# Stores of gates and operands begun by GpSimd, and feed-forward quarters in alternating direction with four pieces kept

## The chip, the cores and the metric

The kernel runs on one core of a Trainium2 chip. The metric is device time in microseconds (us), and the time of a version is the median of its runs. One further execution was recorded by the hardware profiler, and all views below are of that one. The engines are PE (TensorE), DVE (VectorE), ACT (ScalarE), POOL (GpSimd) and SP (SyncE, which in the version before begins every data transfer). Each engine executes its own instructions strictly in order: an instruction that waits holds up all those behind it on the same engine.

## The reference, cut to what matters

```python
# q, k, v: (8, 8, 576, 64); 4608 tokens of 512 features after the heads are joined
scores = matmul(q_c, k_c.T) / sqrt(64)          # chunks of 64 tokens
attn = exp(scores - max); attn /= sum + 1e-9
x = matmul(attn, v_c)                            # -> (8, 576, 512)
xn = (x - mean) / sqrt(var + 1e-6) * g_ln
x2 = x + maximum(xn @ w_ch1, 0) @ w_ch2          # 512 -> 2048 -> 512
gate = sigmoid(causal_conv(x2, conv_w))          # 5 taps, each feature by itself
out = (gate * (x2 @ w_val)) @ w_out
```

## The kernel before, in words

The 4608 tokens are worked in nine blocks (`b` = 0 to 8) of 512, and attention in 36 units of 128 tokens. The feed-forward layer's 2048 inner features are four quarters (`g`) of 512. Blocks 0 and 1 go through it in the plain way. From block 2 on (`hidden`) a quarter's first layer is done in seven products (called "2", "1", "6", "5", "3", "7", "4") of sums of a quarter of the weights with sums of the activations, which takes the place of eight plain products. A product is twelve matmuls at L1255 (`twelve`). The seven accumulate in two PSUM banks: 1, 6, 7 and 4 in bank a, which the instruction lists name m1, and 2 in bank b, which is then opened anew for 5 and 3 (m2 and m5). Between certain products ACT copies a bank (L1347) or DVE adds one to a copy (L1354): product 6 waits for the copy after 1, product 3 for the one after 5, product 4 for DVE's sum after 7. The second layer's matmuls (L1412 to L1414, called y groups here, three matmuls of 512 columns each) are independent of these and fill the time in between, as do the attention units' bursts (L631) and transposes (L604).

The sums of the weights are made once, written to HBM (`a_dram[g, m]`, 512 KB each) and loaded again for each block (L1327): 7 blocks x 4 quarters x 7 pieces = 196 loads, into a ring of six rooms (`RING`). A load waits until the product six before it has read its room.

After a block's feed-forward layer, `conv` computes the gate's five taps for four groups of 128 features, on ACT (the first, L1638) and DVE (four, L1645), in two rooms u0 and u1 (`u_room`). Each result is stored to HBM (`gate_dram`, L1658) and its room is used again two groups later. `seven` splits the block's output into seven operands for the later gated projection, on ACT (L1472) and DVE (L1477), in three rooms (`SPLITS`), and stores each to `x7_dram` (L1482). These stores are begun by SP, the engine that begins the loads of pieces. `conv_again` and `seven_again` do the same for block 0 out of x2 stored earlier (L1600, L1525).

The order on every engine is set before the launch by a small planner (`Plan.run`): each operation has an engine, a duration and a priority (`pri`), is offered when its predecessors are done, and the engine takes the one with the lowest number. A successor is offered after the planner's `HOP` of the engine (3500 ns for SP, 200 for POOL) plus the operation's `more`, and, where the predecessor ran on SP, plus the successor's own `slack`. These figures decide the order alone; on the chip the instructions wait on semaphores. POOL before has little to do: an attention unit's 1/sqrt(variance) (`rstd`, L770), on which DVE's normalisation (L789) and then PE's transposes (L604) wait, and some copies (L826).

Of the kernel before, what the change touches and what calls it, by code (L numbers as in the profile page):

```python
# [31 lines left out]
class Plan:  # L32
# [23 lines left out]
    def run(self):  # L56
        for op in self.ops:
            op.left = len(op.deps)
            for d in op.deps:
                d.after.append(op)  # L60
        free = {e: 740.0 if e == "SP" else 0.0 for op in self.ops for e in op.eng}
        ready = {e: [] for e in free}
        events = []
        done = set()

        def offer(op):
            for e in op.eng:
                heapq.heappush(ready[e], (op.pri, op.seq, op))

        for op in self.ops:  # L70
            if not op.left:
                offer(op)
        t, n, moved, landed = 0.0, 0, 0.0, []
        while n < len(self.ops):
            for e in free:
                if free[e] > t:
                    continue
                q = ready[e]
                while q and q[0][2].seq in done:
                    heapq.heappop(q)  # L80
                if not q:
                    spent = self.idle(t) if self.idle and e == "PE" else None
                    if spent:
                        free[e] = t + spent
                        heapq.heappush(events, (free[e], -1, None))
                    continue
                op = heapq.heappop(q)[2]
                done.add(op.seq)
                dur = op.dur[op.eng.index(e)] if isinstance(op.dur, tuple) else op.dur
                end = t  # L90
                for x, parts in op.xfer or ():
                    flying = landed[-self.LANES :]
                    if len(flying) == self.LANES:
                        end = max(end, flying[0][0])
                    for l, _ in flying:
                        if sum(m for z, m in flying if z > end) + parts > self.RING:
                            end = max(end, l)
                    turn = self.TURN if parts == P and landed and landed[-1][1] != P else 0.0
                    end += dur
                    moved = max(end + self.LAG, moved + turn) + x  # L100
                    landed.append((moved, parts))
                if not op.xfer:
                    end = t + dur
                free[e] = end
                if len(op.eng) > 1:
                    op.fn(e)
                else:
                    op.fn()
                n += 1
                for a in op.after:  # L110
                    if op.xfer:
                        wait = moved - end
                    else:
                        wait = 0.0 if a.eng == (e,) else max(self.HOP[e], self.HOP["PE"] if "PE" in a.eng else 0.0) + op.more
                        if e == "SP":
                            wait += a.slack
                    a.ready = max(a.ready, end + wait)
                    a.left -= 1
                    if not a.left:
                        heapq.heappush(events, (a.ready, a.seq, a))  # L120
                heapq.heappush(events, (free[e], -1, None))
            if n == len(self.ops):
                break
            t = max(t, events[0][0])
            while events and events[0][0] <= t:
                op = heapq.heappop(events)[2]
                if op is not None:
                    offer(op)
# [3 lines left out]
def chunk_attention_ffn_gated_conv(  # L132
# [1176 lines left out]
        last = [s6, s5, split("7", q12, t3, t2), split("4", q21, t4), t1, t4]  # L1309
        hold("xs", *last)  # L1310

    def hidden(b, g):

        n = NG * (b - SB) + g
        pri = when[b, 4 * g] - 9000.0
        ta, tb = f"h{n % 2}", f"h{1 - n % 2}"
        opens, closes = g == 0, g == NG - 1
        st, w = {}, {}
        two_f = 2 * P

        def product(m, into, new, deps):
            rt = RING[ring_n[0] % len(RING)]
            ring_n[0] += 1

            def load():
                w[m] = slot(rt, [P, 2, 2, two_f], F32R, f"a{b}_{g}_{m}")
                nc.sync.dma_start(out=w[m].bitcast(F32), in_=a_dram[g, m].bitcast(F32))  # L1327

            def go():
                if new:  # L1330
                    st[into] = bank(tb if into == "b" else ta, f"m{m}_{b}_{g}").rearrange("p (f x) -> p f x", f=2)
                x = operand(m)
                twelve(st[into], lambda s, k: w[m][:, s, k], lambda s, k: x[:, s, k], new)

            at = pri + 1400.0 * MS.index(m)
            ld = add("SP", 1300, load, [a_store[g, m]] + take(rt), at - 16000.0)
            ld.more = 1500.0
            o = add("PE", 1410, go, [ld, B_op[b, m]] + deps, at)
            hold(rt, o)
            if g == NG - 1:  # L1340
                hold(f"o{m}", o)
            return o

# [11 lines left out]

            return add("DVE", 700, go, deps, pri - 1e7)

        m2 = product("2", "b", True, take(tb))
        m1 = product("1", "a", True, take(ta))
        s1 = shot("a", "hh0", m1)  # L1360
        c11 = join("hh0", "b", ALU.add, s1, m2)
        m6 = product("6", "a", False, [m1, s1])
# [69 lines left out]
    def seven(b, quad, reads, pri):  # L1432

        st, last = {}, {}
        HB = NB // 2

        def mix(to, x, y, *deps):


            def side(q):
                return [(0, HB, st["t"][:, :, :HB])] if q is None else list(quad(*q))

            def go():
                if "t" not in st:
                    st["t"] = slot("hl1", [P, 2, HB], F32, f"t{b}")
                many = side(x) if x else side(y)
                for lo, hi, _ in many:
                    o, p, r = (  # L1450
                        [a for l, h, a in side(q) if (l, h) == (lo, hi)] or [st["t"][:, :, lo:hi]]
                        for q in (to, x, y)
                    )
                    nc.vector.tensor_tensor(out=o[0], in0=p[0], in1=r[0], op=ALU.subtract)

            o = add("DVE", 760, go, list(deps), pri)
            for q in (x, y):
                if q:
                    last.setdefault(q, []).append(o)
            return o  # L1460

        def split(i, m, src, *deps):
            rt, sp = SPLITS[n_split[0] % 3], {}
            n_split[0] += 1

            def sources():
                return quad(*src) if src else [(0, HB, st["t"])]

            def high():
                sp["t"] = slot(rt, [P, 2, 2, HB], F32R, f"x7_{b}_{m}")  # L1470
                for lo, hi, a in sources():
                    nc.scalar.activation(out=sp["t"][:, 0, :, lo:hi], in_=a, func=AF.Copy)  # L1472

            def low():
                t = sp["t"]
                for lo, hi, a in sources():
                    nc.vector.tensor_tensor(  # L1477
                        out=t[:, 1, :, lo:hi], in0=a, in1=t[:, 0, :, lo:hi].bitcast(F32), op=ALU.subtract
                    )

            def store():
                nc.sync.dma_start(out=x7_dram[b, m].bitcast(F32), in_=sp["t"].bitcast(F32))  # L1482

            oh = add("ACT", 680, high, list(deps) + take(rt), pri)
            ol = add("DVE", 690, low, [oh], pri)
            x7_store[b, m] = add("SP", 1300, store, [ol], pri)
            x7_store[b, m].more = 2000.0
            hold(rt, x7_store[b, m])
            if src:
                last.setdefault(src, []).append(ol)  # L1490
            return ol

        return mix, split, last
# [18 lines left out]
    def seven_again():  # L1512
# [7 lines left out]
        def load(q, room, *deps):  # L1520
# [4 lines left out]
                nc.sync.dma_start(out=st[q], in_=x2_dram[:, 2 * kh : 2 * kh + 2, HB * h : HB * (h + 1)])  # L1525

            o = add("SP", 1300, go, [x2_store[0], *deps], pri)
            o.more = 1500.0
            return o

        mix, split, _ = seven(0, quad, None, pri)
# [39 lines left out]
    def conv_again(f):  # L1571
# [25 lines left out]
            return go  # L1597

        def keep():
            nc.sync.dma_start(out=gate_dram[0][:, f], in_=st["acc"][:, :NB])  # L1600

        pri = when[4 + f, KF // 2]
        ox = add("SP", 1300, load, [x2_store[0]] + take(rt), pri - 8000.0)
# [2 lines left out]
        for i in reversed(range(P0)):  # L1606
            oa = add("DVE", 760, more(i), [oa], pri)
        hold(rt, oa)
        conv_store[0, f] = add("SP", 728, keep, [oa], pri)
        hold(at, conv_store[0, f])  # L1610

    def conv(b):
# [19 lines left out]
        for f in range(KD if b else 0):  # L1632
# [22 lines left out]

            def keep(f=f, st=st):
                for lo, hi, c in segs:
                    nc.sync.dma_start(  # L1658
                        out=gate_dram[b][:, f, lo:hi], in_=st["acc"][:, c - P0 : c - P0 + hi - lo]
                    )  # L1660

# [1 line left out]
            for i in range(1, KT):  # L1663
                oa = add("DVE", 760, more(i), [oa], pri)
            last.append(oa)
            conv_store[b, f] = add("SP", 728, keep, [oa], pri)
            hold(at, conv_store[b, f])
        if b == 0:
            x2_store[b] = add("SP", 2900, store, done, pri)
# [441 lines left out]
```

## Time and profile before

| | us |
|---|---|
| median of 3 runs | 1068.37 |
| lowest, highest | 1067.21, 1068.66 |
| the profiled execution's own time | 1070.03 |
| its span, from the first to the last instruction | 1068.2 |
| PE busy | 1053.9 (99%) |
| DVE busy | 856.4 (80%) |
| ACT busy | 540.3 (51%) |
| POOL busy | 40.4 (4%) |

Busy is the time in which an engine has at least one instruction under way. Matmuls are pipelined, so a busy PE is not a PE at its peak, but time in which PE is not busy is time in which it waits for something. In the rows below a releaser after "<-" is what ended a wait. "DMA late_a<-a" is a load of a piece, "gd" is `gate_dram`, "x7d" is `x7_dram`, SPq is SP's sequencer.

### The profile page before, as it was taken

The numbers are of one execution on the slowest core, as the hardware profiler recorded it, in microseconds if no ns is written. First come the engines' busy times: TensorE is split into PE (matmuls) and PEld (weight loads), VectorE is DVE, ScalarE is ACT, GpSimd is POOL, SyncE is SP. The second block draws the span as 40 slices with busy tenths as digits, with TensorE's granted clock in tenths as the row PEclk, the third lists the DMA queues.
The fourth block names the chain that finished last, engine by engine and source line by source line (L and its number), as shares of the span: only waits on it lengthen the run. The fifth ranks groups of instructions, "written<-read, shape, count | busy, mean of one in ns | idle before, by whom it ended". The sixth has DMA issues, their size and how long they took to land.

```text
span 1068.2 us, 22725 instructions
## 1 busy us (share of the span) xinstructions
PE 1053.9 (99%) x8950; PEld 951.4 (89%) x8950; DVE 856.4 (80%) x1464; ACT 540.3 (51%) x871; POOL 40.4 (4%) x77
## 2 busy tenths in 40 slices
PE   9999999999999999999999999999999999999998
PEld 8988888888899988889888898899898989999998
DVE  5888978888885888767878877878756889998785
ACT  5796634435354445445445543544443555655553
POOL 1011000000000000000000000000000000000000
PEclk9999999999999999999999999999999999999999
DMA  8995358667999899989989989998976988999852
GB/s 193 289 368 175 108 159 252 220 179 207 246 329 270 233 297 337 282 242 344 278 260 329 299 233 233 352 282 250 319 234 203 381 330 305 309 334 377 316 206 80
DMA packets 205905, 284.14 MB, mean 266 GB/s; under 512 B 99278, under 2 KB 151014, under 8 KB 205798
## 3 DMA queue, kind: packets, MB, share of 16 engines
q1 hardware_dynamic: 205798, 282.68, 84.6%
q8 instruction: 71, 1.16, 0.5%
q14 instruction: 36, 0.29, 0.1%
HBM read 207.64 MB, written 67.63 MB: 258 GB/s over the span
## 4 chain that ended last, share of the span: by engine, by line
PE 88%; DMA 4%; issue 2%; DVE 2%; ACT 2%; SPq 1%; POOL 0%; DVEq 0%; ACTq 0%; POOLq 0%
PE m L1255 24%; PE o L1255 8%; PE v L1255 8%; PE y L1034 7%; PE yA L1412 5%; PE yA L1414 5%; PE yB L1412 5%; PE yB L1414 4%; PE yA L1413 4%; PE yB L1413 4%; PE att L631 3%; PE att L604 3%; PE h L1010 3%; PE h L1012 2%; PE h L1011 2%
## 5 line engine op out<-in xcount | busy, mean ns | idle before, releaser
L1255 PEld LDWEIGHTS m<-late,late_a 128*128 128x128 f32 x2352 | 296.3, 188 | 22.5 <-DVE c_hl L1354 6.1
L1255 PE MATMUL m<-late,late_a 128*128 128x256 f32 x2352 | 303.3, 280 | 7.1 <-DMA late_a<-a 3.1
L1645 DVE SCALAR_TENSOR_TENSOR u_room<-X,cw_sb,u_room 128x516 f32<-128x516 f32 (+1 forms) x128 | 95.1, 747 | 10.4 <-ACT u_room L1638 7.9
L1034 PE MATMUL y<-hh,w 128*128 128x512 f32 x224 | 70.9, 398 | 0.0
L1354 DVE TENSOR_TENSOR c_hh<-c_hh,m 128x512 f32<-128x512 f32 x56 | 38.4, 685 | 36.6 <-PE m L1255 22.9
L1347 ACT ACTIVATE c_hh<-m 128x512 f32<-128x512 f32 x56 | 33.4, 596 | 54.9 <-PE m L1255 54.7
L1412 PE MATMUL yA<-late_h,w 128*128 128x512 f32 x148 | 59.4, 401 | 0.0
L1412 PE MATMUL yB<-late_h,w 128*128 128x512 f32 x148 | 59.0, 399 | 0.0
L1414 PE MATMUL yB<-late_h,w 128*128 128x512 f32 x148 | 58.1, 393 | 0.0
L1414 PE MATMUL yA<-late_h,w 128*128 128x512 f32 x148 | 58.0, 392 | 0.0
L1413 PE MATMUL yA<-late_h,w 128*128 128x512 f32 x148 | 58.0, 392 | 0.0
L1413 PE MATMUL yB<-late_h,w 128*128 128x512 f32 x148 | 57.8, 390 | 0.0
L1034 PEld LDWEIGHTS y<-hh,w 128*128 128x128 f32 x224 | 40.8, 188 | 8.4
L1287 ACT ACTIVATE late<-xs 128x512 fp32r<-128x512 f32 x49 | 30.4, 628 | 35.1 <-PE m L1255 20.6
L1010 PE MATMUL h<-xnt,w 128*128 128x512 f32 x112 | 45.4, 405 | 0.0
L770 POOL TENSOR_TENSOR rstd<-ve,neg_half 128x1 f32<-128x1 f32 x36 | 24.7, 687 | 541.8 <-DVE ve L750 541.4
L1012 PE MATMUL h<-xnt,w 128*128 128x512 f32 x112 | 44.2, 395 | 0.0
L1011 PE MATMUL h<-xnt,w 128*128 128x512 f32 x112 | 44.2, 394 | 0.0
L1034 PE MATMUL y<-hl,w 128*128 128x512 f32 x112 | 44.0, 393 | 0.0
L1382 ACT ACTIVATE late_h<-c_hh 128x512 fp32r<-128x512 f32 x38 | 23.9, 630 | 38.9 <-DVE c_hh L1354 38.2
L678 ACT ACTIVATE p<-p 128x512 f32<-128x512 f32 x33 | 20.8, 630 | 41.6 <-DVE p L670 23.6
L699 ACT ACTIVATE pT<-px 128x1024 uint16<-128x1024 uint16 x28 | 38.5, 1374 | 6.3 <-DMA px<-ps 6.1
(272 smaller groups left out, 2440.0 us busy)
## 6 DMA issues: line engine op xcount, KB each, us to landing
late_a<-a SPq DMA_DIRECT2D x196, 512.0 KB, 5.6
x7d<-late_x SPq DMA_DIRECT2D x42, 512.0 KB, 5.9
late_a<-x7d SPq DMA_DIRECT2D x39, 512.0 KB, 5.4
raw<-in_moe_w_ch_dram SPq DMA_DIRECT2D x32, 512.0 KB, 7.6
late<-x7d SPq DMA_DIRECT2D x24, 512.0 KB, 5.5
qk_room<-in_q_dram SPq DMA_DIRECT2D x100, 112.0 KB, 5.2
qk_room<-in_k_dram SPq DMA_DIRECT2D x100, 112.0 KB, 4.1
x7d<-x SPq DMA_DIRECT2D x21, 512.0 KB, 5.6
```

Source lines behind the costliest of these rows:

```text
L699: nc.scalar.activation(out=t.bitcast(U16).rearrange("p (x s) -> p s x", s=2), in_=st["turned"], func=AF.Copy)
L1010: nc.tensor.matmul(ps, wh, xh, start=(kk == 0), stop=False)
L1011: nc.tensor.matmul(ps, wh, xl, start=False, stop=False)
L1012: nc.tensor.matmul(ps, wl, xh, start=False, stop=(kk == KD - 1))
L1034: nc.tensor.matmul(ps, w[:, s], x, start=opens and n == 0, stop=closes and n == 2, skip_group_check=not b)
L1255: nc.tensor.matmul(ps[:, f], l, right(r, k), start=new and f == k == i == 0, stop=k == 1 and i == 2, skip_group_check=True,)
L1347: nc.scalar.activation(out=st[tag], in_=st[into], func=AF.Copy)
L1354: nc.vector.tensor_tensor(out=st[tag], in0=st[tag], in1=y, op=op)
L1412: nc.tensor.matmul(ps, wh, hh, start=opens and f == 0, stop=False)
L1413: nc.tensor.matmul(ps, wl, hh, start=False, stop=False)
L1414: nc.tensor.matmul(ps, wh, hl, start=False, stop=closes and f == 3)
L1645: nc.vector.scalar_tensor_tensor(out=a, in0=X[b][:, f, i : i + L], scalar=cw_sb[:, i, f : f + 1], in1=a, op0=ALU.mult, op1=ALU.add,)
```

## The change

All 127 stores of gates and operands (60 at L1658, 4 at L1600, 63 at L1482) are begun by GpSimd in place of SP. The planner books them on POOL with 640 ns each, counts 5000 ns (gates) or 5800 ns (operands) until they have landed, and gives `slack` after POOL's operations too; `seven_again`'s loads get a `slack` of 1500.

Every second block walks its quarters from 3 down to 0, so that a block begins with the quarter with which the one before it ended. The pieces 5, 3, 7 and 4 of that quarter stay in their rooms and are not loaded again: 6 boundaries x 4 = 24 loads fewer, 172 in place of 196. A list of free rooms (`free_rooms`) takes the place of the fixed ring.

```diff
-                        if e == "SP":
+                        if e in ("SP", "POOL"):
                             wait += a.slack
...
-    def hidden(b, g):
+    KEPT = "5374"
+    kept, free_rooms = {}, list(RING)
+
+    def hidden(b, j):
 
-        n = NG * (b - SB) + g
-        pri = when[b, 4 * g] - 9000.0
+        n = NG * (b - SB) + j
+        g = j if (b - SB) % 2 == 0 else NG - 1 - j
+        ranks = "2165374"
+        pri = when[b, 4 * j] - 9000.0
...
         def product(m, into, new, deps):
-            rt = RING[ring_n[0] % len(RING)]
-            ring_n[0] += 1
+            held = kept.pop(m, None)
+            if held:
+                rt, ld, w[m] = held
+            else:
+                rt = free_rooms.pop(0)
...
-            at = pri + 1400.0 * MS.index(m)
-            ld = add("SP", 1300, load, [a_store[g, m]] + take(rt), at - 16000.0)
-            ld.more = 1500.0
+            at = pri + 1400.0 * ranks.index(m)
+            if not held:
+                w[m] = [None]
+                ld = add("SP", 1300, load, [a_store[g, m]] + take(rt), at - 16000.0)
+                ld.more = 1500.0
+            if j == NG - 1 and b + 1 < NBLK and m in KEPT:
+                kept[m] = rt, ld, w[m]
+            else:
+                free_rooms.append(rt)
...
             def store():
-                nc.sync.dma_start(out=x7_dram[b, m].bitcast(F32), in_=sp["t"].bitcast(F32))
+                nc.gpsimd.dma_start(out=x7_dram[b, m].bitcast(F32), in_=sp["t"].bitcast(F32))
 
             oh = add("ACT", 680, high, list(deps) + take(rt), pri)
             ol = add("DVE", 690, low, [oh], pri)
-            x7_store[b, m] = add("SP", 1300, store, [ol], pri)
-            x7_store[b, m].more = 2000.0
+            x7_store[b, m] = add("POOL", 640, store, [ol], pri)
+            x7_store[b, m].more = 5800.0
...
-            o.more = 1500.0
+            o.more, o.slack = 1500.0, 1500.0
...
             def keep(f=f, st=st):
                 for lo, hi, c in segs:
-                    nc.sync.dma_start(
+                    nc.gpsimd.dma_start(
                         out=gate_dram[b][:, f, lo:hi], in_=st["acc"][:, c - P0 : c - P0 + hi - lo]
                     )
...
-            conv_store[b, f] = add("SP", 728, keep, [oa], pri)
+            conv_store[b, f] = add("POOL", 640, keep, [oa], pri)
+            conv_store[b, f].more = 5000.0
```

The planner is run anew with these figures, so the order moves on every engine from block 2 on. What follows shows three places.

SP in block 6, where the pieces of quarter 2 end and those of quarter 3 begin; a3_1 is piece 1 of quarter 3, gd5 the gates and x7d5 the operands of block 5. Before:

```order
L1327 DMA late_a2_0_2_2135<-a2_4_206 128x1024
L1658 DMA gd5_80<-u_room_185 128x320
L1658 DMA gd5_80<-u_room_185 128x192
L1482 DMA x7d5_5_123<-late_x7_1_1_3132 128x1024
L1482 DMA x7d5_2_120<-late_x7_1_1_3132 128x1024
L1327 DMA late_a2_0_2_2135<-a3_2_207 128x1024
L1658 DMA gd5_80<-u_room_185 128x320
L1658 DMA gd5_80<-u_room_185 128x192
L1327 DMA late_a2_0_6_2162<-a3_1_208 128x1024
```

SP at the same place of the change:

```order
L1335 DMA late_a2_0_2_2135<-a2_7_205 128x1024
L1335 DMA late_a2_0_6_2162<-a3_2_207 128x1024
L690 DMA_TRANSPOSE px31_7889<-ps31_7855 128x8x128
L1335 DMA late_a2_0_6_2162<-a2_4_206 128x1024
L1335 DMA late_a2_0_3_2489<-a3_1_208 128x1024
L563 DMA qk_room_148<-in_q_dram 32x4x224 x4
L1335 DMA late_a2_0_3_2489<-a3_6_209 128x1024
```

The stores are gone from ahead of the loads, and loads follow loads, a crossbar transpose of attention and its inputs.

SP at the start of block 3, which before begins with quarter 0 and loads all seven of its pieces:

```order
L1327 DMA late_a2_0_3_2489<-a0_2_186 128x1024
L1327 DMA late_a2_0_3_2489<-a0_1_187 128x1024
L563 DMA qk_room_148<-in_q_dram 32x4x224 x4
L1327 DMA late_a2_0_2_2135<-a0_6_188 128x1024
L563 DMA qk_room_148<-in_k_dram 32x4x224 x4
L1327 DMA late_a2_0_2_2135<-a0_5_189 128x1024
L1327 DMA late_a2_0_6_2162<-a0_3_190 128x1024
L591 DMA v17_3994<-in_v_dram 64x4x64 x4
L1327 DMA late_a2_0_6_2162<-a0_7_191 128x1024
```

SP at the same place of the change, where block 3 begins with quarter 3:

```order
L1335 DMA late_a2_0_3_2489<-a3_1_208 128x1024
L563 DMA qk_room_148<-in_q_dram 32x4x224 x4
L563 DMA qk_room_148<-in_k_dram 32x4x224 x4
L591 DMA v17_3969<-in_v_dram 64x4x64 x4
L1335 DMA late_a2_0_3_2489<-a2_2_200 128x1024
L690 DMA_TRANSPOSE px17_4051<-ps17_4012 128x8x128
L1335 DMA late_a2_0_3_2489<-a3_6_209 128x1024
```

Pieces 2, 1 and 6 of the quarter are loaded and the four others are not; piece 6 stands behind piece 2 of the next quarter, since its room is that of piece 2 of its own quarter.

PE in the second quarter of block 4, around product 3 (the row named m5) and products 7 and 4 (named m1). Before:

```order
L1412 MATMUL yB_4_5322<-late_h2_1_0_3257,w6_849 128x512
L1413 MATMUL yB_4_5322<-late_h2_1_0_3257,w6_849 128x512
L1414 MATMUL yB_4_5322<-late_h2_1_0_3257,w6_849 128x512
L1255 MATMUL m5_4_1_5503<-late1_2982,late_a2_0_2_2135 128x256 x12
L1255 MATMUL m1_4_1_5425<-late1_2982,late_a2_0_6_2162 128x256 x12
L1255 MATMUL m1_4_1_5425<-late2_3004,late_a2_0_6_2162 128x256 x12
```

PE at the same place of the change:

```order
L1255 MATMUL m5_4_1_5504<-late1_2982,late_a2_0_3_2489 128x256 x12
L1430 MATMUL yB_4_5370<-late_h2_1_0_3257,w6_849 128x512
L1431 MATMUL yB_4_5370<-late_h2_1_0_3257,w6_849 128x512
L1432 MATMUL yB_4_5370<-late_h2_1_0_3257,w6_849 128x512
L1430 MATMUL yB_4_5370<-late_h2_1_0_3257,w6_849 128x512
L1431 MATMUL yB_4_5370<-late_h2_1_0_3257,w6_849 128x512
L1432 MATMUL yB_4_5370<-late_h2_1_0_3257,w6_849 128x512
L1255 MATMUL m1_4_1_5442<-late1_2982,late_a2_0_2_2135 128x256 x12
L631 MATMUL att23_5582<-v22_5390,pT22_5470 64x64 x16
L631 MATMUL att23_5582<-kT23_5458,qT23_5456 64x64 x16
```

Before, products 3, 7 and 4 follow each other at once. In the change two y groups stand between 3 and 7, and a burst (with one more y group, not shown) between 7 and 4.

## Rows read from the trace of the kernel before

**Rows 1.** The page: busy time, share of the span and count by engine.

```profile
PE 1053.9 (99%) x8950; PEld 951.4 (89%) x8950; DVE 856.4 (80%) x1464; ACT 540.3 (51%) x871; POOL 40.4 (4%) x77
```

**Rows 2.** Windows: stretch, length, busy by engine, PEclk, DMA share, GB/s.

```profile
240.00:260.00 20.00, 18.59 (x181) 16.61 (x180) 15.52 (x26) 12.33 (x22) 0.00 (x0) 1.00 0.61 182
...
345.00:700.00 355.00, 349.22 (x3081) 312.93 (x3081) 287.14 (x500) 168.86 (x271) 14.60 (x23) 1.00 0.96 287
...
700.00:790.00 90.00, 90.00 (x780) 81.27 (x780) 67.68 (x123) 41.62 (x68) 3.67 (x6) 1.00 0.87 268
790.00:878.00 88.00, 88.00 (x562) 79.11 (x561) 67.94 (x113) 42.37 (x69) 0.00 (x0) 1.00 0.84 296
...
1050.00:1069.00 19.00, 14.25 (x124) 14.04 (x123) 9.63 (x15) 5.42 (x9) 0.00 (x0) 0.95 0.31 111
```

**Rows 3.** Timeline of PE: start, length, instruction, [idle before <-releaser].

```profile
396.87 2.98 PE L1255 MATMUL m<-late,late_a 128*128 128x256 f32 x24 [1.61 <-DMA late_a<-a]
...
467.42 1.69 PE L1255 MATMUL m<-late,late_a 128*128 128x256 f32 x12 [0.96 <-DVE c_hl L1354]
...
561.45 1.68 PE L1255 MATMUL m<-late,late_a 128*128 128x256 f32 x12 [0.49 <-DVE c_hh L1354]
563.51 1.68 PE L1255 MATMUL m<-late,late_a 128*128 128x256 f32 x12 [0.38 <-DVE c_hl L1354]
...
656.27 1.65 PE L1255 MATMUL m<-late,late_a 128*128 128x256 f32 x12 [0.78 <-DVE c_hl L1354]
...
678.15 3.06 PE L1255 MATMUL m<-late,late_a 128*128 128x256 f32 x24 [1.46 <-DMA late_a<-a]
```

**Rows 4.** Timeline of SP from 384 us: start, length, transfer begun.

```profile
384.47 1.48 SPq L1327 DMA_DIRECT2D late_a<-a  x1
389.31 0.38 SPq L1525 DMA_DIRECT2D u_room<-x2d  x1
...
390.77 0.42 SPq L1327 DMA_DIRECT2D late_a<-a  x1
```

**Rows 5.** Waits: who waited for whom, us in total, times, longest.

```profile
SPq L1525 <- DMA gd<-u_room: 3.3, 1, 3.3
...
ACT u_room L1638 <- DMA gd<-u_room: 25.8, 10, 5.8
```

**Rows 6.** Chain that ended last, 660 to 679 us: start, length, what.

```profile
661.76 5.23 DMA gd<-u_room
...
667.07 0.74 ACT u_room L1638
...
671.95 6.07 DMA late_a<-a
```

**Rows 7.** From issue to landing at L1327 (pieces), L1482 (operands), L1658 (gates).

```profile
DMA to landing us min/median/max: 3.1/5.6/10.6
...
DMA to landing us min/median/max: 2.8/5.9/9.9
...
DMA to landing us min/median/max: 2.5/4.7/7.6
```

**Rows 8.** Timelines of POOL, DVE and PE around 661 us; the normalisation's group, 250 to 860.

```profile
661.06 0.55 POOL L770 TENSOR_TENSOR rstd<-ve,neg_half 128x1 f32<-128x1 f32 x1 [25.16 <-DVE ve L750]
...
662.03 0.54 DVE L789 TENSOR_SCALAR xn<-x,mv,rstd 128x512 f32<-128x512 f32 x1
...
663.26 0.60 PE L604 MATMUL att<-ident,x 128*128 128x128 f32 x4
...
L789 DVE TENSOR_SCALAR xn<-x,mv,rstd 128x512 f32<-128x512 f32 x23 | 12.4, 541 | 0.3
```

**Rows 9.** Chain that ended last: four y groups' worth, a product, transposes.

```profile
153.10 2.77 PE y L1034 x12
...
380.61 0.87 PE att L604 x8
...
863.88 1.41 PE m L1255 x12
```

More of the change, by code (lines that the diff above doesn't have):

```diff
@@ L1310, in operands @@
         hold("xs", *last)
-    def hidden(b, g):
-        n = NG * (b - SB) + g
-        pri = when[b, 4 * g] - 9000.0
+    KEPT = "5374"
[5 more added lines that the diff above has]
+        pri = when[b, 4 * j] - 9000.0
         ta, tb = f"h{n % 2}", f"h{1 - n % 2}"
-        opens, closes = g == 0, g == NG - 1
+        opens, closes = j == 0, j == NG - 1
         st, w = {}, {}
@@ L1321, in product @@
         def product(m, into, new, deps):
-            rt = RING[ring_n[0] % len(RING)]
-            ring_n[0] += 1
+            held = kept.pop(m, None)
[3 more added lines that the diff above has]
+                rt = free_rooms.pop(0)
             def load():
-                w[m] = slot(rt, [P, 2, 2, two_f], F32R, f"a{b}_{g}_{m}")
-                nc.sync.dma_start(out=w[m].bitcast(F32), in_=a_dram[g, m].bitcast(F32))
+                w[m][0] = a = slot(rt, [P, 2, 2, two_f], F32R, f"a{b}_{g}_{m}")
+                nc.sync.dma_start(out=a.bitcast(F32), in_=a_dram[g, m].bitcast(F32))
             def go():
@@ L1332, in go @@
                 x = operand(m)
-                twelve(st[into], lambda s, k: w[m][:, s, k], lambda s, k: x[:, s, k], new)
-            at = pri + 1400.0 * MS.index(m)
-            ld = add("SP", 1300, load, [a_store[g, m]] + take(rt), at - 16000.0)
-            ld.more = 1500.0
+                a = w[m][0]
+                twelve(st[into], lambda s, k: a[:, s, k], lambda s, k: x[:, s, k], new)
+            at = pri + 1400.0 * ranks.index(m)
[7 more added lines that the diff above has]
+                free_rooms.append(rt)
             o = add("PE", 1410, go, [ld, B_op[b, m]] + deps, at)
             hold(rt, o)
-            if g == NG - 1:
+            if j == NG - 1:
                 hold(f"o{m}", o)
@@ L1356, in join @@
             return add("DVE", 700, go, deps, pri - 1e7)
-        m2 = product("2", "b", True, take(tb))
-        m1 = product("1", "a", True, take(ta))
+        two = {
+            m: product(m, into, True, take(tag))
+            for m, into, tag in sorted((("2", "b", tb), ("1", "a", ta)), key=lambda x: ranks.index(x[0]))
+        }
+        m2, m1 = two["2"], two["1"]
         s1 = shot("a", "hh0", m1)
@@ L1599, in keep @@
         def keep():
-            nc.sync.dma_start(out=gate_dram[0][:, f], in_=st["acc"][:, :NB])
+            nc.gpsimd.dma_start(out=gate_dram[0][:, f], in_=st["acc"][:, :NB])
         pri = when[4 + f, KF // 2]
@@ L1608, in conv_again @@
         hold(rt, oa)
-        conv_store[0, f] = add("SP", 728, keep, [oa], pri)
+        conv_store[0, f] = add("POOL", 640, keep, [oa], pri)
+        conv_store[0, f].more = 5000.0
         hold(at, conv_store[0, f])
```

## The prediction

> **What bounds the kernel now.** I read the busy times first: PE is busy for 1053.9 of 1068.2 us [rows 1], so 14.3 us is all that any change of order can win, and PE's own work is the same before and after (2555 rows of matmuls in both programs, the same products). The windows say where those 14.3 us lie [rows 2]. The granted clock is 1.00 (the 2.4 GHz level) in each stretch but the very last, so the clock has nothing to give. From 240 to 260 us PE stands for 1.41 us, at the entry to the seven products; the order up to there is the same in both programs. From 1050 to the end it stands for 4.75 us (0.8 of that lies past the span), while the last output is stored; that tail is the same too. Between 700 and 878 us PE never stands: 90.00 of 90.00 and 88.00 of 88.00 us, although the DMA engines are 84 to 87% busy there and SP still begins every store. From 345 to 700 us, blocks 3 to 6, it stands for 355.00 - 349.22 = 5.78 us. These 5.78 us are what the change can win.
>
> The timeline of PE shows them one by one [rows 3]: 1.61 and 1.46 us end with the landing of a piece, and 0.96, 0.49, 0.38 and 0.78 us end with a sum on DVE; together 5.68.
>
> The two late pieces have one story. In the first [rows 4], SP finishes an issue at 384.47 + 1.48 = 385.95 and begins nothing until 389.31. It is held by a load into u_room (L1525) that waits 3.3 us for a gate store to land [rows 5]. A pair of gate stores follows, and only then, at 390.77, the piece, on which PE's product at 396.87 waits. In the second, the chain of waits [rows 6] runs from a gate store (5.23 us to land) to ACT's scaling of the same room at 667.07, DVE's four taps, the next gate store on SP, and the piece behind it at 671.95, which takes 6.07 us to land, against a median of 5.6 [rows 7]. So the pieces were not unusually slow in flight. They were begun late, because SP stood before a store or a load of the side work. The four waits on DVE come where products stand together without a y group between, as in the order of block 4.
>
> **The change, part by part.**
>
> *Stores leave SP.* 127 transfers go, and 994 become 843 with the 24 loads. The pair ahead of a3_1 in block 6, on which 1.46 us hang, is gone, so I count 1.46 as won. At the first place the gate stores are gone as well, but the load of L1525 stays on SP and waits for a gate store still. The planner books that store as taking longer than before and the load with 1.5 us of slack, so the load stands later in the order; I count 1.61 as won, with 0 as the other end. Together -3.07, between -1.46 and -3.07.
>
> *PE's order.* Products 3, 7 and 4 of block 4's second quarter now have y groups or a burst between them, and in block 5's second step I find the same: two y groups after 5 and after 3. That is where 0.96, 0.49 and 0.38 us were lost: -1.83. In block 6 products 7, next 1 and 4 still stand together around a burst, as at 656.27, so 0.78 stays. The other end is 0: the same adjacency remains at some nine places, of which before three lost time.
>
> *What a store begun by GpSimd costs.* The trace has none, so I bound it. Its issue: from below SP's 0.38 us [rows 4], from above three of GpSimd's own operations, 3 x 0.55 [rows 8], about 1.6. GpSimd is idle for 96% of the span [rows 1], so the issue costs nothing by itself. What waits behind it on that engine is `rstd`. At 661 us it ends at 661.61, DVE's normalisation begins at 662.03 and ends at 662.57, PE's transposes begin at 663.26 [rows 8]: 0.42 + 0.69 = 1.1 us pass before PE would stand. A store of 0.4 to 0.6 us directly ahead fits in that, and one of 1.6 would cost 0.5. There are 23 such steps; if a quarter met a store of 1.6 us, 3 us. I take 0.3.
>
> Its landing: from below SP's fastest, 2.5 us, from above SP's slowest, 9.9 [rows 7]. What waits for it are rooms: ACT's scaling of u_room, which before already waited 25.8 us in ten times [rows 5], and the operands' three rooms. The order allows 0.64 + 0.2 + 5.0 = 5.84 us for gates and 6.64 for operands, where it allowed 4.2 and 6.8. SP's medians of 4.7 and 5.9 [rows 7] fit in that. I take the medians, so no cost, and give the upper end to a rival.
>
> DVE's normalisation, a scaling from SBUF to SBUF, takes 541 ns and 12.4 us in all [rows 8], 2% of the 610 us of that window. The Trainium skill speaks against the move (SBUF — State Buffer, the box on DVE blocking a DMA in SBUF: two separate sides): a transfer begun by GpSimd stands while DVE runs a copy or a scaling that takes the port which the two share, since its descriptors can't be written, and a DMA of about 620 ns becomes one of about 3100. By it a store that collides would land 2.5 us later, by the row at most 0.54 us later, and 2% of the stores collide; nothing in the sum hangs on it.
>
> *Four pieces kept.* A load of 512 KB (0.524 MB) at the 287 GB/s of 345 to 700 us is 1.83 us of the DMA engines, and 24 of them 44 us, some 7% of their time in blocks 3 to 8. PE did not stand at 84 to 87% of share [rows 2], so less traffic by itself gives PE nothing; it shortens landings in a stretch that had 96%. I count 0.
>
> The price is in the rooms. Where four of six are held, piece 6 of a block's first quarter takes the room of piece 2 of the same quarter, two products back in place of six. Its load can begin only when product 2 has ended. In the new order of block 3 there stand between the two: transposes (0.87), six y groups of 2.77 / 4 = 0.69 each, product 5 (1.41) and one more y group [rows 9]: 0.87 + 4.15 + 1.41 + 0.69 = 7.1 us; at the other boundaries it is much the same. Against it stand an issue of 0.42 [rows 4] and a landing of 5.6 [rows 7]: 1.1 us to spare. With the slowest landing, 10.6, PE would stand for 3.9. Six boundaries, most within the spare time: I take 0.7 in all, with 0 and 6 x 2.0 = 12 (half of the way to the slowest, each time) as ends.
>
> **Sum.** -3.07 - 1.83 + 0.3 + 0.7 = -3.9 us. The span becomes 1064.3, and the profiled execution's own time 1070.03 - 3.9 = 1066.1. That execution lay 1.66 above the median of the runs, 1068.37; the median becomes 1064.5, 0.36% less. About 0.2% (2.1 us) is what a measurement of this kernel can tell from no change.
>
> **The rivals.**
>
> *The win is eaten at the boundaries and by the rest.* If only 1.46 is won on SP (the load of L1525 holds SP as before), half of 1.83 on PE, and piece 6 costs 0.4 at each of six boundaries, the sum is -1.46 - 0.9 + 2.4 = 0: 1068.4. For it speaks that a spare 1.1 us is less than the spread of landings, 3.1 to 10.6 [rows 7]; against it, that there are fewer transfers in flight just there.
>
> *The move does not do what it is made for.* If pieces are late because the 16 DMA engines are full (96% from 345 to 700 us, [rows 2]) and not because SP stands, both waits on pieces stay, and only the 1.83 and the shorter queue give: 1068.37 - 1.83 + 1.0 = 1067.5. Against it speak SP's 3.3 us without an issue [rows 4, 5]. The Trainium skill has this rule (DMA: Bandwidth & Descriptors, Issuing engines are not separate DMA queues): starting DMAs from several engines saves only the time of the issue. The rule does not speak of waits on SP.
>
> *Slower: stores land later than the order allows.* The place is ACT, which stands at a room's reuse while the copies of the banks wait behind. There are 2 reuses of u0 and u1 in each of 7 blocks and 4 of the operands' rooms in each of 8 rounds, 46. Before, 25.8 us of such waits [rows 5] went with at most 0.96 + 0.49 + 0.38 + 0.78 = 2.6 us of PE [rows 3], so PE loses between 0 and 10% of what ACT waits; I take 6%. If every reuse waits 2.9 us (the way from the gates' median to their slowest, [rows 7]), that is 133 us on ACT and 8 on PE: with the -3.9 it gives 1072.5. It decides from about 1.4 us per reuse, a landing of some 7.2 us for gates. For it speaks that the largest of SP's landings (7.6 and 9.9) lie beyond that; against it, that a store begun elsewhere no longer stands behind 512 KB loads in SP's queue.
>
> **How the numbers follow.** I give my forecast 0.58, with its own range 1062 to 1066; the win eaten 0.18; the move without effect 0.07; slower 0.17. From these: faster by over 0.2% 0.60, within 0.2% 0.23, slower by over 0.2% 0.17. The lowest time is all 5.78 won, 1062.6, with 2 us for what shorter queues may give elsewhere: 1060.5. The highest takes in the slower case: 1072.5.
>
> **What would show it.** Right: no wait of PE on late_a in blocks 3 to 6; no gap in SP's issues from a gate store; PE full from 700 us on as before; stores on POOL that land in 4 to 7 us. In the first quarters of blocks 3 to 8, product 6 shows whether its load is late. ACT's waits on gd and x7d below 26 us would show that rooms come free in time. Wrong: DVE waiting for `rstd`, ACT at L1657 waiting for stores for more than some 60 us, or PE standing before product 6.

## The result, and the profile after

The changed kernel takes 1079.64 us (median of 4 runs, 1076.72 to 1082.86) against 1068.51 for the kernel before in the same comparison: a ratio of 1.0106, 95% interval 1.0075 to 1.0137. It is slower by 1.1%; the forecast was 0.36% faster. The profiled execution took 1080.24 us with a span of 1078.5, 10.3 us more than before.

The first line of the page divides these 10.3 us (busy us, share of the span, instructions):

```profile
PE 1057.8 (98%) x8950; PEld 954.3 (88%) x8950; DVE 857.1 (79%) x1464; ACT 540.8 (50%) x871; POOL 108.6 (10%) x204
```

Against [rows 1] PE is busy for 3.9 us longer with the same matmuls, and stands for 20.7 us in place of 14.3, 6.4 more. The windows show where (length, busy us of PE and how many matmuls, then PEld, DVE, ACT, POOL; last the granted clock, the DMA share, GB/s):

```profile
345.00:700.00 355.00, 351.79 (x3164) 316.44 (x3163) 288.88 (x503) 169.71 (x274) 51.27 (x92) 1.00 0.91 272
...
790.00:878.00 88.00, 83.27 (x514) 74.17 (x514) 62.80 (x104) 39.98 (x65) 8.62 (x16) 0.98 0.74 262
...
835.00:843.00 8.00, 4.57 (x20) 3.94 (x20) 5.80 (x12) 5.47 (x10) 0.13 (x1) 0.80 1.03 416
...
996.00:1005.00 9.00, 8.64 (x61) 8.64 (x62) 5.75 (x9) 3.05 (x6) 0.00 (x0) 0.81 0.62 209
...
960.00:1050.00 90.00, 85.76 (x726) 85.34 (x725) 66.43 (x104) 46.41 (x81) 3.72 (x7) 0.98 0.80 283
```

From 345 to 700 us PE stands for 3.21 us, where it stood for 5.78 [rows 2]: 2.57 are won, and none of the six stalls of [rows 3] is left. The loss lies behind, where PE never stood before: 4.73 us from 790 to 878 and 4.24 from 960 to 1050. Before, the second of these windows reads

```profile
960.00:1050.00 90.00, 90.00 (x780) 89.99 (x779) 68.89 (x108) 48.24 (x84) 0.00 (x0) 1.00 0.75 272
```

The waits of PE and ACT say for whom (us in total, times, longest):

```profile
PE m L1255 <- DVE c_hl L1369: 3.4, 1, 3.4
PE v L1255 <- ACT v_hh L1909: 3.3, 1, 3.3
PE m L1255 <- DMA late_a<-a: 2.7, 2, 1.5
...
ACT u_room L1657 <- DMA gd<-u_room: 22.7, 11, 3.2
ACT pT L699 <- DMA px<-ps: 17.4, 9, 3.5
ACT late_x L1490 <- DMA x7d<-late_x: 14.2, 8, 2.9
ACT x L1490 <- DMA x7d<-x: 14.0, 6, 3.4
```

Two single waits make up 6.7 us of PE. ACT's waits for gates (`gd`) fell from 25.8 [rows 5] to 22.7 us; those for operands (`x7d`, the reuse of a room at L1490) are 28.2 in fourteen times. Before they were 3.1 in four:

```profile
ACT late_x L1472 <- DMA x7d<-late_x: 2.4, 3, 1.1
ACT x L1472 <- DMA x7d<-x: 0.7, 1, 0.7
```

Between issue and landing of operands (L1500) and gates (L1677) lie

```profile
DMA to landing us min/median/max: 3.4/7.2/13.6
...
DMA to landing us min/median/max: 2.0/5.2/9.8
```

against 2.8/5.9/9.9 and 2.5/4.7/7.6 [rows 7]. How an operand's store becomes PE's wait stands in the chain that ended last, around 838 us (start, length, what):

```profile
822.22 13.55 DMA x7d<-x
835.78 0.02 issue
835.80 0.02 ACTq L1490
835.81 0.04 issue
835.86 0.72 ACT x L1490 x2
836.58 0.53 ACT late_h L1400
837.11 0.02 issue
837.13 0.69 DVE late_h L1403
837.82 0.61 DVE c_hl L1369
838.43 0.04 issue
838.48 1.68 PE m L1255 x11
```

The store is the third of three that GpSimd began within 1.2 us. ACT stands for its room with the split of the next operand, and behind it on ACT is `late_h`, on that DVE's `late_h`, and behind that on DVE the join for which product 4 waits. PE's timeline (start, length, in brackets the idle time and what ended it):

```profile
833.43 1.61 PE L1255 MATMUL m<-late,late_a 128*128 128x256 f32 x12 [1.20 <-DMA late_a<-a]
838.48 1.89 PE L1255 MATMUL m<-late,late_a 128*128 128x256 f32 x12 [3.43 <-DVE c_hl L1369]
840.17 0.63 PE L1430 MATMUL yA<-late_h,w 128*128 128x512 f32 x1
840.60 0.63 PE L1431 MATMUL yA<-late_h,w 128*128 128x512 f32 x1
...
843.39 0.40 PE L1432 MATMUL yB<-late_h,w 128*128 128x512 f32 x1
843.62 0.40 PE L1430 MATMUL yB<-late_h,w 128*128 128x512 f32 x1
```

Behind the stand of 3.43 us the matmuls of 512 columns begin 0.43 us apart, and from 843.39 again 0.23: the granted clock of 835 to 843 is 0.80, so that part of it passed at the lower level, 1.2 in place of 2.4 GHz. At 996.36 PE stands for 3.34 us, and the clock of 996 to 1005 is 0.81 (ACT, then PE):

```profile
994.71 0.60 ACT L2006 ACTIVATE os<-o 128x512 f32<-128x512 f32 x1 [4.32 <-DMA out_dram<-os]
...
996.36 2.64 PE L1255 MATMUL v<-late_a,wv_sums 128*128 128x256 f32 x12 [3.34 <-ACT v_hh L1909]
```

Here the wait just ahead of it is another: ACT stands for a store of the output, which was begun at 985.36 and took 9.26 us. Only further back does the chain hold an operand's store of 9.20 us from 969.52, for which ACT's split at 978.80 waited 2.68 us. What the clock lacks in the two stretches, 8 x 0.20 + 9 x 0.19 = 3.3 us, is most of PE's 3.9 us of longer busy time.

### The profile page after: what moved, and what is told of

Read it like the earlier page. It is cut to its first block, busy times and chain, and to the rows that moved or that the text cites. A ratio compares the mean times of both kernels' runs of the same rounds, so it can differ in the third digit from the quotient of the medians.

```text
span 1078.5 us, 22758 instructions
## 1 busy us (share of the span) xinstructions
PE 1057.8 (98%) x8950; PEld 954.3 (88%) x8950; DVE 857.1 (79%) x1464; ACT 540.8 (50%) x871; POOL 108.6 (10%) x204
## 3 DMA queue, kind: packets, MB, share of 16 engines
q0 software_dynamic: 12400, 42.48, 10.2%
## 4 chain that ended last, share of the span: by engine, by line
PE 85%; DMA 8%; DVE 3%; ACT 2%; SPq 1%; issue 1%; POOL 0%; ACTq 0%; POOLq 0%
PE m L1255 22%; PE y L1034 7%; PE v L1255 7%; PE o L1255 7%; PE yA L1430 4%; PE yB L1430 4%; PE yB L1432 4%; PE yA L1432 4%; PE yB L1431 4%; PE yA L1431 4%; PE att L631 3%; PE att L604 3%; PE h L1010 3%; PE h L1012 2%; PE h L1011 2%; DMA px<-ps 2%
## 5 line engine op out<-in xcount | busy, mean ns | idle before, releaser
L1677 POOL DMA_DIRECT2D gd<-u_room x60 | 33.0, 553 | 232.4 <-DVE u_room L1664 232.2
L699 ACT ACTIVATE pT<-px 128x1024 uint16<-128x1024 uint16 x28 | 38.5, 1376 | 17.6 <-DMA px<-ps 17.4
L1291 DVE TENSOR_TENSOR late<-xs,late 128x512 fp32r<-128x512 f32 x49 | 32.8, 686 | 12.2 <-ACT late L1287 12.1
```

The source lines that it names most:

```text
L699: nc.scalar.activation(out=t.bitcast(U16).rearrange("p (x s) -> p s x", s=2), in_=st["turned"], func=AF.Copy)
```

## The experiments

Ratios are against the kernel before on the same chip, with 95% intervals. **Theory A**: GpSimd's stores land late. **Theory B**: the quarters and kept pieces cost the time. **Theory C**: the order that the plan makes once GpSimd is free for every store is at fault. **Theories D and E** stand at their runs.

**One part at a time.** `e1` is the kernel before with the stores of the change alone, `e2` the changed kernel with all stores on SP under the old figures, `e3` the changed kernel with the operands' stores back on SP:

```diff
-                nc.gpsimd.dma_start(out=x7_dram[b, m]...
+                nc.sync.dma_start(out=x7_dram[b, m]...
-            x7_store[b, m] = add("POOL", 640, store, [ol], pri)
-            x7_store[b, m].more = 5800.0
+            x7_store[b, m] = add("SP", 1300, store, [ol], pri)
+            x7_store[b, m].more = 2000.0
```

> The kernel before with only the stores of gates and operands begun by GpSimd (and the planner's figures for them); order of quarters and rings of pieces as before. Theory A (a store of an operand that GpSimd begins lands late, ACT stands at the reuse of its room, and PE stands behind ACT): 1074 to 1081 us, ACT waits for x7d over 15 us, the slowest landing of an operand over 11 us. Theory B (the alternating quarters and the kept pieces cost the time): 1064 to 1069 us.

> The changed kernel with all stores begun by SP again, under the figures of before; the quarters alternate and four pieces are kept. Theory A: 1063 to 1069 us, ACT waits for x7d under 5 us, PE has no gap over 2.5 us behind the copies or joins of the products. Theory B: 1074 to 1081 us.

> The changed kernel with only the operands' stores back on SP (1300, 2000 in the plan); gates stay on GpSimd. Theory A, where the operands' landings are the cause: 1063 to 1069 us, ACT waits for x7d under 5 us. If the gates' stores are the cause as well (their rooms, ACT at the gates' first tap): 1071 to 1078 us. Theory B: 1074 to 1081 us.

Measured: `e1` 1.0052 (1.0028 to 1.0076; 1076.4 us), ACT's waits for x7d 27.5 us; `e2` 0.9999 (0.9974 to 1.0023); `e3` 0.9961 (0.9942 to 0.9981), waits for x7d 6.7. Theory B falls, since the quarters and kept pieces alone cost nothing, and so do the gates as a cause. But the stores alone make only about half of the change's loss (1.0052 against 1.0106). Each version is planned anew, and the parts don't simply add up. With the operands left on SP the change is a gain of 0.4%, what I had forecast for the whole. `e1`'s slowest landing of an operand, 11.2 us, is theory A's number.

**Engine or order.** `e4` keeps the changed kernel's plan and lets SP begin every store (only `nc.gpsimd` becomes `nc.sync`). `e5` keeps the plan of `e3` and lets GpSimd begin the operands' stores (only `nc.sync` becomes `nc.gpsimd` in `store`). PE, DVE and ACT have the same order within each pair.

> The changed kernel in exactly its own order on PE, ACT, DVE, with each of the stores begun by SP at the place in the program where GpSimd began it. Theory A (the landing of GpSimd's stores): landings of operands return to a median near 5.9 us and none over 11 us, ACT waits for x7d under 10 us, 1065 to 1071 us, the rest from SP standing at stores again. Theory C (the order that the plan makes out of the new figures is at fault, not the engine that begins the stores): 1075 to 1082 us, with the gaps of PE at the same two products.

> PE, ACT and DVE in exactly the order of the kernel that has only the gates' stores on GpSimd (which was 0.4% faster than before); the operands' stores are planned on SP as there, but begun by GpSimd. Theory C (the order that the plan makes when GpSimd is free for every store is at fault: ACT is booked too early for a room's reuse): ratio 0.993 to 0.999, ACT waits for x7d under 12 us. Theory A (the landing of stores that GpSimd begins is at fault in any order): ratio 1.003 to 1.010, ACT waits for x7d over 20 us.

| order planned with operands' stores on | begun by SP | begun by GpSimd |
|---|---|---|
| SP | 0.9961 (0.9942 to 0.9981), `e3` | 0.9980 (0.9959 to 1.0000), `e5` |
| POOL | 1.0123 (1.0092 to 1.0155), `e4` | 1.0106 (1.0075 to 1.0137), the change |

The rows differ by 1.3 to 1.6%, the columns by 0.2%, within the intervals. Theory A, that a store begun by GpSimd costs the time in any order, falls with `e5`: it isn't slow, although its operands take

```profile
DMA to landing us min/median/max: 3.1/6.9/13.0
```

`e4` is as slow as the change, and slower than either theory's number (its profiled execution, 1077.4 us, is its fastest, the median 1085.3), although its operands land in 2.7/6.3/9.5 us. But it shows less than its time suggests. ACT's waits in it are

```profile
ACT pT L699 <- DMA px<-ps: 31.0, 12, 5.3
ACT late_x L1490 <- DMA x7d<-late_x: 11.0, 9, 2.0
ACT x L1490 <- DMA x7d<-x: 9.8, 6, 2.6
```

and theory C's gaps at the same two products are only in part there. PE's longest stand lies behind a wait for px, a crossbar transpose that SP begins (ACT, then PE):

```profile
416.31 1.34 ACT L699 ACTIVATE pT<-px 128x1024 uint16<-128x1024 uint16 x1 [4.90 <-DMA px<-ps]
...
418.14 2.93 PE L1255 MATMUL m<-late,late_a 128*128 128x256 f32 x12 [3.24 <-ACT c_hl L1362]
```

Near 838 PE stands for 1.89 us, for a piece and not for the join; near 995 the stand behind the output's store is left, 2.16 us. The waits for px were 17.4 us in the change, when SP had no stores to begin. So the two slow times of the lower row have different stands in the traces, and `e4` can't tell what the change's order would cost with nothing but faster landings.

GpSimd's stores do land later, by 0.7 us at the median in one order (6.9 against 6.2 in `e3`), and that costs nothing that these intervals show. The Trainium skill (DMA: Bandwidth & Descriptors, Latency and other measured facts) gives about 1 us to the first byte by GpSimd against 0.6 by SP; the sign agrees, and up to the landing, under this load, the difference is 0.7.

How the plan moved ACT can be worked out from the traces: from the end of DVE's part of a split to the moment at which ACT comes to the split three later, into the same room (its start less the idle time before it), over the some 40 such pairs less than 25 us apart. The median is 12.2 us before, 12.8 in `e3`, 12.2 in `e5`; 10.2 in the change, 9.9 in `e4`, 9.7 in `e1`. Among these six the slow ones are those where ACT comes 2 us sooner. In the runs below it is 11.1 in `e7`, 15.9 in `e8`, 13.7 in `e9` and 15.3 in `e10`, and `e10` is slow all the same: the median goes with the booked figure, but does not decide the time.

**Gates alone.** `e6` is the kernel before with the gates' stores alone on GpSimd.

> The kernel before with only the gates' stores begun by GpSimd; quarters, rings and operands' stores as before. If the gain of that change is SP's, freed of the gates' stores: ratio 0.994 to 0.998. If it needs the kept pieces and the new order of quarters as well: 0.999 to 1.003.

Measured: 0.9980 (0.9966 to 0.9995). That part is a gain by itself; whether the kept pieces add to it (0.9961) is within the intervals.

**The booking.** `e7`, `e8` and `e11` are the changed kernel with another figure for the operands' landing in the plan:

```diff
-            x7_store[b, m].more = 5800.0
+            x7_store[b, m].more = 8000.0    # e7; 12000.0 in e8, 16000.0 in e11
```

> The changed kernel with the operands' stores booked at 8000 in place of 5800 ns of landing. Theory C: ACT is booked 2.2 us later for each room, waits for x7d fall from 28 to under 18 us, ratio 1.000 to 1.006. Theory A: little change, 1.006 to 1.013. Theory D (SP's loads run ahead in the plan, so ACT stands at pT for px whatever is booked for the stores): waits for x7d fall but 15 to 18 us of waits for px stay, and the ratio stays over 1.004.

> As the run before, with 12000 ns. Theory C: waits for x7d under 6 us, ratio 0.994 to 1.002. Theory A: over 1.006, since the slowest landing of 13.6 us is still beyond the booking and PE stands at the same two places. Theory D: waits for px of 15 us or more stay, ratio over 1.004.

> The changed kernel with 16000 ns booked for every operand's store, above the slowest landing seen (14.9 us). Theory C: ACT waits for x7d under 6 us, ratio 0.993 to 1.000; if the operands are then written too late for the loads of the products, a stand of PE on late_a at the blocks' start and 1.002 to 1.010.

Measured: 8000: 1.0064 (1.0042 to 1.0086), waits for x7d 15.3 us; 12000: 0.9986 (0.9966 to 1.0005), 18.0 us; 16000: 1.0189 (1.0158 to 1.0220), none. The time at 8000 is just above theory C's range and inside those of A and D, whose 15 to 18 us of waits for px are there too (17.5), so `e7` separates nothing. The time at 12000 is theory C's alone, but the waits are not: I expected under 6 us. So the sum of ACT's waits doesn't measure the harm. Theory D falls with `e8`, which keeps 12.3 us of waits for px and isn't slow, where `e10` below has 12.1 and is. The time at 16000 was in nobody's numbers: no operand's room is waited for at all, and PE stands for other work that came late, most at one place (PE, then DVE, in the trace of `e11`):

```profile
917.16 2.50 PE L1255 MATMUL o<-w,late_h 128*128 128x256 f32 x10 [6.22 <-DVE late_h L1933]
...
909.08 2.77 DVE L1738 TENSOR_TENSOR sums<-w 128x256 f32<-128x256 f32 x8
911.76 2.14 DVE L1744 TENSOR_TENSOR sums<-sums 128x512 f32<-128x512 f32 x3
913.81 2.09 DVE L1764 TENSOR_TENSOR late_wo<-sums,late_wo 128x256 fp32r<-128x256 f32 x6
```

DVE makes sums of weights there, ahead of the operand for which PE waits. Why the plan came to this order with that figure I did not follow.

**The two places.** `e9` books 12000 for the operands of the last two blocks alone, and `e10` for all others alone:

```diff
-            x7_store[b, m].more = 5800.0
+            x7_store[b, m].more = 12000.0 if b > 6 else 5800.0    # e9; the two exchanged in e10
```

> The changed kernel with 12000 in place of 5800 ns booked for the operands' stores of the last two blocks' operands only (7 and 8, written from 820 us on); the order is the changed kernel's own up to there. Theory C, at the two places of the profile (838 and 996 us, each with a stretch at the lower clock behind it): most of the loss goes, ratio 0.999 to 1.004, no gap of PE over 2.5 us after 800 us. Theory E (the loss is spread over all blocks and the two places are those of one execution): ratio 1.005 to 1.010.

> The reverse: 12000 ns for the operands' stores of blocks 0 to 6, 5800 for the last two. Theory C at the two places: the stands near 838 and 996 us stay, ratio 1.004 to 1.010. Theory E: about half of the loss goes, 1.002 to 1.006; if the early stands (416 and 438 us) are the whole of it, 0.998 to 1.002.

Measured: `e9` 1.0007 (0.9987 to 1.0026), `e10` 1.0082 (1.0055 to 1.0108). Most of the loss hangs on the booking of the last two blocks' operands, as theory C said, and theory E falls. `e9` shows the mechanism most purely, since up to 820 us its order is the changed kernel's. Its three stores of 820.9 to 822.1 land as late,

```profile
DMA to landing us min/median/max: 9.7/11.5/13.5
```

but ACT now does first what PE waits for (timeline of ACT in `e9`):

```profile
830.17 0.63 ACT L1400 ACTIVATE late_h<-c_hh 128x512 fp32r<-128x512 f32 x1 [1.90 <-DVE c_hh L1369]
832.89 0.63 ACT L1400 ACTIVATE late_h<-c_hl 128x512 fp32r<-128x512 f32 x1 [2.08 <-DVE c_hl L1369]
834.38 0.60 ACT L1362 ACTIVATE c_hh<-m 128x512 f32<-128x512 f32 x1 [0.86 <-PE m L1255]
834.87 0.62 ACT L1490 ACTIVATE late_x<-t 128x512 fp32r<-128x512 f32 x1
836.17 0.71 ACT L1490 ACTIVATE x<-X 128x384 fp32r<-128x384 f32 x2
```

In the changed kernel the same timeline reads:

```profile
835.86 0.72 ACT L1490 ACTIVATE x<-X 128x384 fp32r<-128x384 f32 x2 [3.30 <-DMA x7d<-x]
836.49 0.61 ACT L1400 ACTIVATE late_h<-c_hh 128x512 fp32r<-128x512 f32 x1
838.46 0.63 ACT L1400 ACTIVATE late_h<-c_hl 128x512 fp32r<-128x512 f32 x1 [1.36 <-DVE c_hl L1369]
```

The same two kinds of instruction have changed places, and PE stands for 0.55 us there, not 3.43. In `e10` the split stands ahead as in the change, the third store takes 14.04 us, and PE stands for 4.7 us.

The order alone doesn't make this stand. In `e5` the split stands ahead of the same `late_h` too (ACT, then PE):

```profile
830.19 0.72 ACT L1490 ACTIVATE x<-X 128x384 fp32r<-128x384 f32 x2 [1.84 <-DMA x7d<-x]
830.82 0.62 ACT L1400 ACTIVATE late_h<-c_hh 128x512 fp32r<-128x512 f32 x1
...
832.82 1.65 PE L1255 MATMUL m<-late,late_a 128*128 128x256 f32 x12 [1.43 <-DVE c_hl L1369]
```

There the store is the second of its three and lands after 11.07 us, against 13.55 in the change; ACT comes to the room 9.3 us after its issue (10.3 in the change), PE stands for 1.43 us, and the granted clock of 818 to 845 is 1.00. So the loss at this place takes both, the split ahead of PE's work and the late landing.

The second place did not stay in `e10`, as I had expected: with the same order on ACT, and 2.57 us of waiting for the operand's room, ACT stood only 1.82 us for the output's store and PE 0.84. How much of the change's 3.34 us there is owed to the operand's room is therefore not shown.

**A version to keep.** `e12` is `e3` with the operands' stores booked at 4000 in place of 2000 on SP.

> The kernel with only the gates' stores on GpSimd (0.9961), its operands' stores on SP booked at 4000 in place of 2000 ns. If ACT's remaining 6.7 us of waits for x7d cost PE anything (1.85 us near 830): 0.992 to 0.996; if not: 0.996 to 0.999.

Measured: 0.9983 (0.9962 to 1.0004); the remaining waits (3.4 us) cost nothing that shows. `e3`, at 0.9961, is the best version measured and beats both kernels; its interval overlaps those of `e5`, `e6`, `e8` and `e12`.

## Why the prediction was wrong

**Where it was right.** Both late pieces are gone, and so are the waits on DVE of block 4: 2.57 us won from 345 to 700, in place of the 4.9 less 0.7 that I put there. New stands there, 1.6 us for a copy on ACT at 415.95 (behind a wait of ACT for px) and 1.5 for a piece at 437.95, took the rest. The second is the boundary's price: product 6 of block 4's first quarter waits 1.50 us for its piece. One such place in six boundaries: 0.7 in all was too little by 0.8. `rstd` behind stores cost PE nothing, against 0.3. The kept pieces and the new direction of the quarters together gave nothing by themselves (`e2`), where I counted 0 and 0.7. (The 44 us of loads saved are 8% of the 533 us from 345 to 878, not 7; nothing hung on that.)

**The step that failed** is "The order allows 0.64 + 0.2 + 5.0 = 5.84 us for gates and 6.64 for operands, where it allowed 4.2 and 6.8 ... I take the medians, so no cost". For gates it holds (`e3`, `e6`). For operands the landing was put at no cost, and it had one. Their median came to 7.2 us, over the 6.64 allowed, and the three begun at 821 us took 9.8 to 13.6. ACT stood 28.2 us for their rooms, against 3.1, with work of PE behind it: PE stood for 3.43 and 3.34 us at two places where I had it full "from 700 us on as before" (the second behind an output's store, and only in part, as far as is shown, for an operand's), and the clock took 3.3 us more. With nothing changed but 12000 in place of 5800 for the last two blocks' operands, the loss is gone (`e9`, 1.0007); with the reverse most of it stays (`e10`, 1.0082). So the loss hangs on the order that the plan makes with that booking, and not on the engine by itself (`e5`, 0.9980).

Why 6.64 did harm where 6.8 before did none is shown only in part. I took the booked figure for the time that a room really had. But before, a store also waited for its turn on SP among the loads: from the end of DVE's part to the issue 3.9 us on average over the 63 operands, against 0.5 with GpSimd in the change. ACT came back to a room after 12.2 us before and after 10.2 in the change, which fits. It isn't the whole: `e10` is slow at a median of 15.3, and at the place near 838 ACT came later after the store's issue (10.3 us) than in `e5` (9.3), which isn't slow. At that place, the one that the runs take apart, it was settled by what the order puts behind the split and by how late that one store lands; the median distance does not tell that, and why this plan put it so I did not follow.

**The slower rival** had the place (ACT at a room's reuse) and the sign, but rested on the gates and on lateness alone, and its price of 6% was wrong: 25.1 us more of waits for x7d would be 1.5 us. A wait of 3.30 us ended in a stand of 3.43, since ACT and DVE held PE's next operands behind it; one of 2.68, with a late store of the output after it, lies in the chain of the other. And I wrote that "the clock has nothing to give": it can take, 3.3 us here.

**The two rules.** That starting transfers from several engines saves only the time of the issue (the Trainium skill, DMA: Bandwidth & Descriptors, Issuing engines are not separate DMA queues) agrees with the columns of the table, 0.2% either way, most plainly in the upper one of its two rows, since in the lower the stands differ. Of the rule that DVE can hold up a transfer begun by GpSimd (the Trainium skill, SBUF — State Buffer, SBUF: two separate sides) the issue shows nothing: 63 operands' issues took 531 to 570 ns with DVE 79% busy. What it does to the landing no run here separates.

## What to carry to other kernels

A planner's constant for a wait is only part of the real distance between two uses of a buffer; the queue in which the transfer is planned is the other (3.9 us on average before, 0.5 in the change). Whoever moves transfers to an idle engine must read what stands behind the reuse on its engine, and how late the slowest landing comes there, not whether the landing's median fits the constant. 18 us of ACT's waits were free in `e8`; two stands of 3.4 us with the clock behind them are most of 1.1% in the change.

## What the runs showed of the hardware

Three stores of 512 KB that GpSimd began within 1.2 us landed at some 830.8, 833.3 and 835.8 us (9.8, 11.6 and 13.6 after their issue), 2.5 us apart, in the change and alike in `e9`; the same three begun by SP in `e4`, 1.0 us apart, took 7.8 to 9.5 and landed 2.5 and 1.1 us apart. The DMA share was 1.00 from 821 to 836 in the change and 1.02 from 826 to 838 in `e4`: such bursts landed one after another, and whether GpSimd's queue has a part in it is not shown.

The granted clock fell behind stands of PE of 3.43 and 3.34 us in the change. In `e9`, behind a stand of 3.0 us that ended at 415.67, it was 0.86 from 410 to 435; in `e10`, behind one of 2.14 that ended at 416.25, it was 0.93 from 410 to 435; in `e7`, where PE stood for 3.0 us near 991, that of 985 to 1010 stayed at 1.00. The length of the stand alone doesn't decide it in these rows.
